# Linear attention ahead of two dense layers: k's projection in plain float32 by row halves, q's maximum subtracted in SBUF, both heads' attend sums in one PSUM bank, closer ranks of units

## The chip, the cores and the metric

One core of one Trainium2 chip. The metric is the device time of one execution in microseconds; below it is the median of three runs.

## What is computed

The inputs are q, k and v (4 batches, 8 heads, 576 positions, 64 features), a feature map w_phi (64 x 128) and the weights of two dense layers, which the kernel receives as 64-bit floats where the host has them so. The output has 2304 rows of 512.

```python
def phi(x):
    proj = np.einsum('bhsd,df->bhsf', x, w_phi)
    proj = proj - np.max(np.abs(proj), axis=-1, keepdims=True)
    return np.concatenate([np.exp(proj), np.exp(-proj)], axis=-1)
q_p, k_p = (phi(q), phi(k))
kv = np.einsum('bhsf,bhsd->bhfd', k_p, v)
z = np.sum(k_p, axis=2)
num = np.einsum('bhsf,bhfd->bhsd', q_p, kv)
den = np.einsum('bhsf,bhf->bhs', q_p, z)[..., None] + 1e-06
x = num / den                         # heads side by side: 2304 x 512
h = np.maximum(np.maximum(x @ w1, x @ w2), x @ w3) @ w_out
...                                   # then rms norm, silu(xn @ w_gate) * (xn @ w_val), @ w_out
```

## The kernel before, in words

**Units.** A unit is two batches and two heads; there are 8 (`NU`). The transposed k and q of a unit are [128, 1152]: rows 0 to 63 are head 0's features, rows 64 to 127 head 1's, and the columns are the positions of both batches. They are cut in 3 chunks of 384 columns (`C`), or 9 blocks of 128.

**The k side of a unit.** A chunk of k comes by two DMAs: `load_k` (L383) on SP's queue into `kraw`, and `load_kh` (L386) on POOL's queue into `kh`, which is float32r (in unit 0, ACT rounds `kraw` into `kh` instead). DVE makes the rest `kl = kraw - kh` (`rest_k`, L389). `k_proj` (L419) multiplies each block by two wide copies of w_phi, `wbh` and `wbl`, with zeros in the other head's quadrants, as three float32r products (`mm3`); both heads' features land side by side in one PSUM bank, two blocks to a bank (ring `pk`, banks 0 and 1). DVE takes the maximum of the absolute values (`k_max`, L429) and subtracts it (`k_sub`, L435), ACT takes the two exponentials (`k_exp`, L443), and `kv_sum` (L445) adds k_p^T [v, 1] of one head in one bank of ring `pkv` (4 and 5). After the last of the 5 steps of a unit `kv_copy` (L458) moves the sums to SBUF (`kvs`).

**The q side of a unit.** For each of 3 chunks `q_proj` (L490) multiplies the two row halves of `qraw` by w_phi in plain float32, head 0 into bank 2 and head 1 into bank 3 (ring `pq`, two banks). ACT copies both to `pc` in SBUF (`q_copy`, L494), POOL finds the largest absolute value over the partitions (`partition_all_reduce`, L498) into `mq`, and DVE's `q_sub` (L503), one per head, reads the projection in PSUM again and writes the difference over `pc`. ACT takes two exponentials (L511). `attend` (L516), one per head, multiplies them by `kvs` into one bank per head of ring `nd` (banks 6 and 7). DVE adds epsilon, inverts and multiplies (`guard` L527, `invert` L532, `divide` L535), per head; PE turns the result (`turn`, L541; ring `xt`, which is bank 1), ACT rounds it to `xh` (L545), and DVE keeps the rest `xl` (L548). A tile of `xh`, `xl` is 384 positions, all features.

**The dense layers.** 64-bit weights come in pieces of 128 x 512, which ACT, DVE and POOL narrow to float32 and split (lines 636 to 673; the first four pieces, which are those of the first layer's first step, go without POOL). Each product is three float32r products through `mm3` (the matmuls of L369 into `up` and `po`). The first `up` depends on `pqlast` (the last `q_proj`) and on `kdone` (nothing of the k side's buffers is used any more).

**What sets the order.** A planner holds a list of operations, each with an engine, a rank, an estimated duration, what it reads and writes, and the ring of buffers that a tile comes from. It plays them through and issues each engine's instructions in the order of their estimated starts; of those that could start within 0.12 us of each other, the lower rank goes first. Each engine then runs its queue in that order. Unit n's ranks begin at n x `U`, with `U = 22.0`; the q side of a unit stands one `U` behind its k side. The loads of the first four weight pieces are ranked at 62, 88, 114 and 140, apart from `U`; all later work of the dense layers is ranked from `A = NU * U + 24`.

```python
for j, r in enumerate(halves):        # q_proj, before and after
    mm(out=buf(f"pq{n}.{c}.{j}")[:, 0:C], lhsT=wst[r, :], rhs=buf(f"qraw{n}.{c}")[r, :], start=True, stop=True)
nc.vector.tensor_tensor(              # q_sub before: first operand in PSUM
    out=buf(f"pc{n}.{c}")[:, j, :], in0=buf(f"pq{n}.{c}.{j}")[:, 0:C], in1=buf(f"mq{n}.{c}")[:, j, :],
    op=ALU.subtract,
)
```

Of the kernel before, what the change touches and what calls it, by code (L numbers as in the profile page):

```python
# [8 lines left out]
FP32 = mybir.dt.float32  # L9
# [8 lines left out]
P = 128  # L18
# [18 lines left out]
NKP = (NST + 1) // 2  # L37
# [162 lines left out]
R384, R256, R512, FULL, HALF = 0.173, 0.118, 0.229, 0.222, 0.15  # L200
# [4 lines left out]
def attn_moe_kernel(ctx, tc, qT, kT, vv, w_phi, w1, w2, w3, wo1, wg, wv, wo2, rms_g, out):  # L205
# [53 lines left out]
    banks("nd", (6, 7))  # L259
    banks("xt", (1,))  # L260
# [8 lines left out]
    ring("kvs", "attnq", 4, [P, 2, 2, 2 * D])  # L269
    ring("den", "attnq", 4, [P, NSUB])  # L270
# [49 lines left out]
    def clear():  # L320
        nc.vector.memset(eps, 1e-6)
        nc.vector.memset(ones, 1.0)
        nc.vector.memset(zero, 0.0)
        for j, r in enumerate(halves):
            for w in (wbh, wbl):
                nc.vector.tensor_copy(out=w[r, (1 - j) * F:(2 - j) * F], in_=zero[r, :])
# [21 lines left out]
    pl.op("DVE", -99, 1.0, clear, w=["zeros", "ones", "eps", "wk"])  # L348
    pl.op("ACT", -98, 1.4, lambda: nc.scalar.activation(out=eps, in_=eps, func=ACTF.Copy), r=["eps"], w=["eps"])
    for j, r in enumerate(halves):  # L350
        f = slice(j * F, (j + 1) * F)
        pl.op("ACT", -97, act_us(F), lambda r=r, f=f: nc.scalar.copy(out=wbh[r, f], in_=wst[r, :]),
              r=["wphi"], w=["wk"])
        pl.op("DVE", -97, dve_us(F), lambda r=r, f=f: nc.vector.tensor_tensor(
            out=wbl[r, f], in0=wst[r, :], in1=r32(wbh[r, f]), op=ALU.subtract), r=["wphi"], w=["wk"])
# [17 lines left out]
    U = 22.0  # L373
    LOAD = 2.5

    def unit(n):
# [532 lines left out]
```

## Time and profile before

| | us |
|---|---|
| median of 3 runs | 953.73 (952.88 to 954.95) |
| the profiled execution | 950.4 |
| its span, first to last instruction | 948.7 |
| PE busy | 924.8 (97%) |
| DVE busy | 611.0 (64%) |
| ACT busy | 346.9 (37%) |
| POOL busy | 254.3 (27%) |

The busy shares are averages over two stages. The attention takes about the first 180 us; the two dense layers take the rest. PE counts as busy while a matmul is in flight, which includes the pipeline's tail behind the last one of a group.

### The profile page before, as it was taken

Reading aid. Unit: us, or ns where it says so; the run is one execution under the profiler, and the core shown is the slowest. Engines: PE = TensorE matmul, PEld = TensorE weight load, DVE = VectorE, ACT = ScalarE, POOL = GpSimd, SP = SyncE. Lnnn points to the kernel's source line nnn. Section 1 sums busy time; section 2 is a strip of 40 time slices with the busy share of each in tenths; the row PEclk is TensorE's granted clock in tenths of the full one; section 3 lists DMA queues with packets and bytes.
Section 4 is the critical chain, followed back from the end, with each engine's and each line's share of the span. In section 5 each row is a group of like instructions: output and inputs, shape, how many; then the busy total and the mean of one; then the engine's idle time right before and its main releaser. Section 6 shows DMA issues by size and latency. Waiting matters only on the chain.

```text
span 948.7 us, 16696 instructions
## 1 busy us (share of the span) xinstructions
PE 924.8 (97%) x6860; PEld 864.1 (91%) x6860; DVE 611.0 (64%) x1160; ACT 346.9 (37%) x645; POOL 254.3 (27%) x184
## 2 busy tenths in 40 slices
PE   8998888899999999999999999999999999999998
PEld 7877776799999999999999999999999999999997
DVE  6899888478856485848788645555645826633233
ACT  6767676455321222213367433123222222211111
POOL 5444443365321231304253123022222202300000
PEclk9999999799999999999999999999999999999999
DMA  8645531023302021201100210200201201000112
GB/s 221 164 125 135 160 99 63 2 67 90 92 20 67 1 67 45 64 26 45 45 1 22 68 44 24 67 18 28 89 1 45 89 1 45 1 1 1 45 68 89
DMA packets 57005, 55.61 MB, mean 59 GB/s; under 512 B 21856, under 2 KB 52320, under 8 KB 56928
## 3 DMA queue, kind: packets, MB, share of 16 engines
q1 hardware_dynamic: 53904, 50.41, 17.8%
q0 software_dynamic: 3024, 4.13, 1.7%
q8 instruction: 54, 0.88, 0.4%
q14 instruction: 23, 0.19, 0.1%
HBM read 49.81 MB, written 4.72 MB: 57 GB/s over the span
## 4 chain that ended last, share of the span: by engine, by line
PE 80%; DVE 1%; issue 0%
PE up L369 55%; PE po L369 23%; DVE xl L814 1%; PE pn L802 0%; PE nd L525 0%; PE pn L791 0%; DVE acc L715 0%; DVE acc L809 0%; PE pq L492 0%; PE xt L543 0%; DVE pc L504 0%; DVE dg L797 0%; DVE hl L739 0%; DVE hf L755 0%; DVE rc L804 0%
## 5 line engine op out<-in xcount | busy, mean ns | idle before, releaser
L369 PE MATMUL up<-xh,wp 128*128 128x384 f32 x2016 | 541.7, 338 | 0.0
L369 PEld LDWEIGHTS up<-xh,wp 128*128 128x128 f32 x2016 | 367.4, 188 | 3.5 <-issue 0.5
L369 PE MATMUL up<-xl,wp 128*128 128x384 f32 x1008 | 340.1, 337 | 0.0
L369 PEld LDWEIGHTS up<-xl,wp 128*128 128x128 f32 x1008 | 189.2, 188 | 2.9
L671 POOL TENSOR_TENSOR wa<-wa,wp 128x512 f32<-128x512 f32 x56 | 80.8, 1443 | 401.0 <-ACT wp L665 335.2
L836 DVE TENSOR_TENSOR hf<-up,hf 128x384 f32<-128x384 f32 x72 | 40.1, 556 | 167.0 <-PE up L369 166.5
L738 ACT CAST hh<-hf 128x384 fp32r<-128x384 f32 x108 | 55.5, 514 | 233.5 <-DVE hf L836 131.7
L369 PE MATMUL po<-wp,hh 128*128 128x512 f32 x432 | 133.6, 390 | 0.0
L715 DVE TENSOR_TENSOR acc<-po,acc 128x384 f32<-128x384 f32 (+1 forms) x210 | 125.3, 610 | 11.9 <-PE po L369 11.6
L834 ACT ACTIVATE hf<-up 128x384 f32<-128x384 f32 x72 | 35.4, 492 | 162.4 <-PE up L369 162.3
L498 POOL PARTITION_ALL_REDUCE mq<-pc x24 | 67.0, 2790 | 95.3 <-issue 61.8
L369 PEld LDWEIGHTS po<-wp,hh 128*128 128x128 f32 x432 | 80.2, 188 | 11.9
L739 DVE TENSOR_TENSOR hl<-hf,hh 128x384 fp32r<-128x384 f32 x108 | 66.9, 620 | 31.9 <-ACT hh L738 31.8
L755 DVE TENSOR_TENSOR hf<-up,hf 128x384 f32<-128x384 f32 x72 | 40.0, 555 | 72.0 <-PE up L369 71.4
L369 PE MATMUL po<-hh,wp 128*128 128x384 f32 x288 | 85.6, 337 | 0.0
L369 PE MATMUL po<-wp,hl 128*128 128x512 f32 x216 | 84.1, 389 | 0.0
L673 POOL TENSOR_TENSOR wp<-wa,wm 128x512 fp32r<-128x512 f32 x56 | 75.2, 1344 | 15.1 <-DVE wm L657 10.1
L369 PEld LDWEIGHTS po<-hh,wp 128*128 128x128 f32 x288 | 53.4, 188 | 0.3
L657 DVE SCALAR_TENSOR_TENSOR wm<-wst,wm 128x512 f32<-128x512 uint32 x60 | 50.6, 844 | 0.9
L636 ACT ACTIVATE wm<-wst 128x512 f32<-128x512 f32 x60 | 40.4, 674 | 29.2 <-POOL wp L673 18.9
L443 ACT ACTIVATE e<-e 128x512 f32<-128x512 f32 (+1 forms) x80 | 45.8, 593 | 12.9 <-DVE e L435 12.1
L369 PE MATMUL po<-hl,wp 128*128 128x384 f32 x144 | 48.6, 338 | 0.1
(81 smaller groups left out, 1059.3 us busy)
## 6 DMA issues: line engine op xcount, KB each, us to landing
wst<-in_moe_w_dram SPq DMA_DIRECT2D x18, 512.0 KB, 3.5
wst<-in_moe_w_out_dram SPq DMA_DIRECT2D x18, 512.0 KB, 3.6
wst<-in_moe_w_gate_dram SPq DMA_DIRECT2D x12, 512.0 KB, 3.6
wst<-in_moe_w_val_dram SPq DMA_DIRECT2D x12, 512.0 KB, 3.6
kraw<-in_kT_dram SPq DMA_DIRECT2D x24, 192.0 KB, 3.2
qraw<-in_qT_dram SPq DMA_DIRECT2D x24, 192.0 KB, 2.7
out_dram<-acc SPq DMA_DIRECT2D x18, 256.0 KB, 2.0
vt<-in_vv_dram SPq DMA_DIRECT2D x16, 256.0 KB, 4.4
```

Of the source, the lines that this page charges most:

```text
L369: mm(out=ps, lhsT=a, rhs=b, start=start and i == 0, stop=stop and i == n - 1)
L443: nc.scalar.activation(out=dst, in_=src, func=ACTF.Exp, scale=-1.0 if u else 1.0)
L498: nc.gpsimd.partition_all_reduce(buf(f"mq{n}.{c}").rearrange("p a c -> p (a c)"), buf(f"pc{n}.{c}").rearrange("p a c -> p (a c)"), P, bass ...
L636: nc.scalar.activation(out=buf(f"wm{self.id}").bitcast(FP32), in_=self.view()[1].bitcast(FP32), func=ACTF.Abs)
L657: nc.vector.scalar_tensor_tensor(out=mf, in0=lo.bitcast(U32), scalar=2.0 ** -52, in1=mf, op0=ALU.mult, op1=ALU.mult)
L671: eng.tensor_tensor(out=a, in0=a, in1=r32(buf(self.h)), op=ALU.subtract)
L673: eng.tensor_tensor(out=buf(self.l), in0=a, in1=buf(f"wm{self.id}").bitcast(FP32), op=ALU.add)
L715: nc.vector.tensor_tensor(out=acc, in0=p, in1=acc, op=ALU.add)
L738: pl.op("ACT", rank, act_us(C), lambda: nc.scalar.copy(out=buf(h), in_=buf(f)), r=[f], w=[h])
L739: pl.op("DVE", rank + 0.6, dve_us(C) + 0.1, lambda: nc.vector.tensor_tensor(out=buf(l), in0=buf(f), in1=r32(buf(h)), op=ALU.subtract), r=[ ...
L755: pl.op("DVE", w + q, dve_us(C), lambda f=f, p=p: nc.vector.tensor_tensor(out=buf(f), in0=buf(p)[:, 0:C], in1=buf(f), op=ALU.max), r=[p], ...
L836: pl.op("DVE", w + q + 4.1, dve_us(C), lambda f=f, p=ups[1]: nc.vector.tensor_tensor(out=buf(f), in0=buf(p)[:, 0:C], in1=buf(f), op=ALU.mu ...
```

## The change

The diff, cut to what acts. k's wide weights, the zeros and the `kh`/`kl` tiles go, with POOL's DMAs of k and DVE's `rest_k`. `k_proj` takes a chunk of three blocks at a time: for each block and head it multiplies 64 rows of `kraw` by 64 rows of w_phi in plain float32, head 0 into bank 0 and head 1 into bank 1. Maximum, difference and exponentials go by chunk and head (384 columns) where they went by two blocks with both heads (512 columns; the fifth step 256). `q_sub` is one instruction of 768 columns for both heads with both operands in SBUF. Both heads' `attend` write one bank (6 x 65 columns of bank 6), and `guard`, `invert` and `divide` are one each for both heads. `xt` has bank 7 for itself. `kvs` and the v tiles are 65 columns wide instead of 128. Ranks are closer: `U` is 17, and chunks stand U/3 apart.

```diff
-    banks("nd", (6, 7))
-    banks("xt", (1,))
+    banks("nd", (6,))
+    banks("xt", (7,))
...
-    ring("kraw", "attnk", 4, [P, C])
-    ring("kh", "attnk", 6, [P, C], FP32R)
-    ring("kl", "attnk", 3, [P, C], FP32R)
-    ring("mk", "attnk", 3, [P, 4])
-    ring("e1", "attnk", 5, [P, 4, F])
-    ring("e2", "attnk", 5, [P, 4, F])
+    ring("kraw", "attnk", 7, [P, C])
+    ring("mk", "attnk", 4, [P, NSUB])
+    ring("e1", "attnk", 9, [P, NSUB, F])
+    ring("e2", "attnk", 9, [P, NSUB, F])
...
-    U = 22.0
+    U = 17
...
-            if n:
-                pl.op("POOL", rk, 0.75, lambda c=c: load_kh(c), w=[kh], size=P * C * 4, lag=LOAD + 1.0, when=hold)
-            else:
-                pl.op("ACT", rk, act_us(C), lambda c=c: nc.scalar.copy(out=buf(f"kh{n}.{c}"), in_=buf(f"kraw{n}.{c}")),
-                      r=[kr], w=[kh])
-            pl.op("DVE", rk + 14, dve_us(C) + 0.4 * (n > 0), lambda c=c: rest_k(c), r=[kr, kh], w=[kl])
...
-        def k_proj(i):
-            pk = buf(f"pk{n}.{i}").rearrange("p (a f) -> p a f", a=2)
-            for t in range(2 * i, min(2 * i + 2, NST)):
-                c, o = divmod(t * P, C)
-                mm3(pk[:, t % 2, :], [(buf(f"kh{n}.{c}")[:, o:o + P], buf(f"kl{n}.{c}")[:, o:o + P], wbh, wbl)])
+        def k_proj(c):
+            for i in range(NSUB):
+                for j, r in enumerate(halves):
+                    mm(out=k_view(c, j)[:, i, :], lhsT=buf(f"kraw{n}.{c}")[r, i * P:(i + 1) * P], rhs=wst[r, :],
+                       start=True, stop=True)
...
+            pk = [new("pk", f"pk{n}.{c}.{j}") for j in range(2)]
+            pl.op("PE", rk - 8, KPROJ, lambda c=c: k_proj(c), r=["wphi", f"kraw{n}.{c}"], w=pk)
...
-        def q_sub(c, j):
-            nc.vector.tensor_tensor(
-                out=buf(f"pc{n}.{c}")[:, j, :], in0=buf(f"pq{n}.{c}.{j}")[:, 0:C], in1=buf(f"mq{n}.{c}")[:, j, :],
-                op=ALU.subtract,
-            )
+        def q_sub(c):
+            pc = buf(f"pc{n}.{c}")
+            nc.vector.tensor_tensor(out=pc, in0=pc, in1=buf(f"mq{n}.{c}"), op=ALU.subtract)
...
-                        mm(out=nd[r, i, 0:D + 1], lhsT=e[:, j, q], rhs=kvs[:, u, b, 0:D + 1], start=u == 0, stop=u == 1)
+                        mm(out=nd[r, 2 * i + j, :], lhsT=e[:, j, q], rhs=kvs[:, u, b, :], start=u == 0, stop=u == 1)
...
-        def divide(c, j):
+        def divide(c):
             nc.vector.tensor_tensor(
-                out=buf(f"xs{n}.{c}")[:, :, j * D:(j + 1) * D], in0=nd_view(c, j)[:, :, 0:D],
-                in1=bc(buf(f"den{n}.{c}.{j}"), [P, NSUB, D]), op=ALU.mult,
+                out=buf(f"xs{n}.{c}").rearrange("p i (j d) -> p (i j) d", j=2), in0=nd_view(c)[:, :, 0:D],
+                in1=bc(buf(f"den{n}.{c}"), [P, 2 * NSUB, D]), op=ALU.mult,
             )
...
-            rk = base + U + 7.3 * c
+            rk = base + U + U / 3 * c
...
-            for j in range(2):
-                pl.op("DVE", rk - 5, dve_us(C), lambda c=c, j=j: q_sub(c, j), r=[pq[j], mq], w=[f"{pc}:{j}"])
+            pl.op("DVE", rk - 5, dve_us(2 * C), lambda c=c: q_sub(c), r=[mq], w=[f"{pc}:0", f"{pc}:1"])
```

## Rows read from the trace of the kernel before

**Rows 1.** The chain of work that ended last, within the first 185 us: start, duration, engine, tile, line, instructions.
```profile
177.16 0.57 DVE pc L504
177.77 1.37 PE pq L492 x4
179.14 2.29 PE up L369 x12
```

**Rows 2.** Busy time of each engine by stretch of the span (instructions in brackets), granted TensorE clock (1.00 is full speed), DMA share, GB/s.
```profile
core 0: us, PE busy (x) PEld busy (x) DVE busy (x) ACT busy (x) POOL busy (x), PEclk, DMA share, GB/s
30.00:50.00 20.00, 20.00 (x360) 16.22 (x360) 16.14 (x39) 15.11 (x30) 8.65 (x6) 1.00 0.53 136
50.00:75.00 25.00, 23.23 (x404) 18.73 (x399) 22.48 (x54) 17.27 (x35) 12.53 (x7) 1.00 0.53 137
75.00:100.00 25.00, 22.52 (x396) 17.68 (x394) 23.77 (x54) 17.49 (x34) 10.28 (x8) 1.00 0.55 138
100.00:125.00 25.00, 22.59 (x379) 18.45 (x379) 21.29 (x49) 17.32 (x34) 9.95 (x7) 0.93 0.51 142
125.00:150.00 25.00, 21.44 (x412) 17.43 (x410) 23.34 (x58) 18.16 (x35) 11.83 (x6) 1.00 0.22 67
160.00:170.00 10.00, 7.67 (x103) 6.02 (x99) 4.09 (x15) 4.97 (x11) 5.09 (x2) 0.67 0.23 73
180.00:220.00 40.00, 40.00 (x310) 39.37 (x309) 27.57 (x54) 19.61 (x39) 19.75 (x13) 1.00 0.18 54
220.00:900.00 680.00, 679.56 (x3716) 654.81 (x3715) 419.32 (x727) 200.07 (x366) 156.49 (x112) 1.00 0.13 39
```

**Rows 3.** POOL's line 498 (the all-reduce over partitions) and ACT's line 459 (the copies of the k sums, two per unit), all of each: duration in ns min/median/max, start of the first and of the last.
```profile
L498 POOL PARTITION_ALL_REDUCE mq<-pc x24: 2734/2737/3202, 13.6 to 180.9; - x24
L459 ACT COPY kvs<-pkv x16: 361/382/403, 18.1 to 161.1; 128x260 f32<-128x260 f32 x16
```

**Rows 4.** The timeline of one turn of the q loop, behind the last k work: start, duration, instruction, idle time before it and its releaser.
```profile
167.65 2.74 POOL L498 PARTITION_ALL_REDUCE mq<-pc  x1 [3.77 <-ACT pc L495]
170.43 1.02 DVE L504 TENSOR_TENSOR pc<-pq,mq 128x384 f32<-128x384 f32 x2 [0.16 <-POOL mq L498]
171.21 1.93 PE L492 MATMUL pq<-qraw,wst 64*128 64x384 f32 x4
173.38 0.84 ACT L495 COPY pc<-pq 128x384 f32<-128x384 f32 x2
174.38 2.74 POOL L498 PARTITION_ALL_REDUCE mq<-pc  x1 [3.99 <-ACT pc L495]
```

**Rows 5.** The timeline of PE: a `q_proj` with both heads, and the first and the last of the six matmuls of one `k_proj` step (two blocks).
```profile
85.01 0.92 PE L492 MATMUL pq<-qraw,wst 64*128 64x384 f32 x4
...
92.75 0.38 PE L369 MATMUL pk<-wbh,kh 128*128 128x256 f32 x1
...
93.44 0.28 PE L369 MATMUL pk<-wbh,kl 128*128 128x256 f32 x1
```

**Rows 6.** Groups of DVE instructions of the first 215 us, shapes apart: count, busy us, mean ns of one, idle time before them.
```profile
L390 DVE TENSOR_TENSOR kl<-kraw,kh 128x384 fp32r<-128x384 f32 x24 | 13.6, 568 | 1.3 <-ACT kh L412 1.1
L429 DVE TENSOR_REDUCE mk<-pk 128x4 f32<-128x512 f32 x32 | 21.7, 685 | 7.1 <-PE pk L369 6.5
L429 DVE TENSOR_REDUCE mk<-pk 128x2 f32<-128x256 f32 x8 | 3.3, 416 | 1.9 <-PE pk L369 1.9
L435 DVE TENSOR_TENSOR e<-pk,mk 128x512 f32<-128x512 f32 x32 | 21.6, 683 | 0.2
L504 DVE TENSOR_TENSOR pc<-pq,mq 128x384 f32<-128x384 f32 x48 | 24.5, 549 | 2.8 <-POOL mq L498 2.8
L528 DVE TENSOR_SCALAR den<-nd 128x3 f32<-128x3 f32 x48 | 7.3, 153 | 15.5 <-PE nd L525 15.4
L533 DVE RECIPROCAL den<-den 128x3 f32<-128x3 f32 x48 | 7.7, 170 | 0.5
L536 DVE TENSOR_TENSOR xs<-nd,den 128x192 f32<-128x192 f32 x48 | 16.0, 351 | 0.5
```

**Rows 7.** Groups of ACT's and POOL's instructions of the first 215 us, in the same columns.
```profile
L443 ACT ACTIVATE e<-e 128x512 f32<-128x512 f32 x64 | 39.5, 635 | 7.4 <-DVE e L435 6.8
L443 ACT ACTIVATE e<-e 128x256 f32<-128x256 f32 x16 | 6.8, 424 | 5.5 <-DVE e L435 5.3
L387 POOL DMA_DIRECT2D kh<-in_kT_dram x21 | 11.9, 567 | 0.0
```

**Rows 8.** The timeline at the start of the attention: k's first chunk rounded, its rest, the first `k_proj`.
```profile
4.69 0.99 ACT L412 CAST kh<-kraw 128x384 fp32r<-128x384 f32 x2 [0.84 <-DMA kraw<-in_kT_dram]
5.24 1.04 DVE L390 TENSOR_TENSOR kl<-kraw,kh 128x384 fp32r<-128x384 f32 x2 [1.06 <-ACT kh L412]
5.40 0.56 PE L369 MATMUL pk<-wbh,kh 128*128 128x256 f32 x1
```

**Rows 9.** The timeline at two places where DVE met an all-reduce, and the spread of durations of four DVE lines (min/median/max ns, start of the first and of the last).
```profile
50.07 2.73 POOL L498 PARTITION_ALL_REDUCE mq<-pc  x1 [4.09 <-issue]
50.23 2.05 DVE L651 SCALAR_TENSOR_TENSOR wa<-wst,wm 128x512 int32<-128x512 int32 x1
...
109.60 2.73 POOL L498 PARTITION_ALL_REDUCE mq<-pc  x1 [4.59 <-issue]
109.62 2.18 DVE L673 TENSOR_TENSOR wp<-wa,wm 128x512 fp32r<-128x512 f32 x1
...
L651 DVE SCALAR_TENSOR_TENSOR wa<-wst,wm x6: 676/688/2047, 50.2 to 153.3; 128x512 int32<-128x512 int32 x6
L673 DVE TENSOR_TENSOR wp<-wa,wm x4: 674/1254/2182, 65.4 to 143.6; 128x512 fp32r<-128x512 f32 x4
L390 DVE TENSOR_TENSOR kl<-kraw,kh x24: 540/549/780, 5.2 to 142.1; 128x384 fp32r<-128x384 f32 x24
L504 DVE TENSOR_TENSOR pc<-pq,mq x46: 539/548/559, 16.3 to 177.6; 128x384 f32<-128x384 f32 x46
```

**Rows 10.** The timeline of PE: the loads of weights and the matmuls of another `q_proj`, whose two banks came free one after the other; each line of loads is one row half's two.
```profile
91.44 0.29 PEld L492 LDWEIGHTS pq<-qraw,wst 64*128 64x128 f32 x2 [1.14 <-DVE pc L504]
91.45 1.37 PE L492 MATMUL pq<-qraw,wst 64*128 64x384 f32 x4 [1.00 <-DVE pc L504]
91.91 0.29 PEld L492 LDWEIGHTS pq<-qraw,wst 64*128 64x128 f32 x2 [0.17 <-DVE pc L504]
```

More of the change, by code (lines that the diff above doesn't have):

```diff
@@ L322, in clear @@
         nc.vector.memset(ones, 1.0)
[L323 to L326, printed above, removed]
     def identity():
@@ L347, in attn_moe_kernel @@
     pl.op("PE", -101, 4.0, wake, r=["ones2"], w=[new("nd", "wake")])
-    pl.op("DVE", -99, 1.0, clear, w=["zeros", "ones", "eps", "wk"])
+    pl.op("DVE", -99, 0.3, clear, w=["ones", "eps"])
     pl.op("ACT", -98, 1.4, lambda: nc.scalar.activation(out=eps, in_=eps, func=ACTF.Copy), r=["eps"], w=["eps"])
[L350 to L355, printed above, removed]
     for i in range(2):
@@ L428, in k_max, with k_view @@
-        def k_max(i, nt):
+        def k_proj(c):
[3 more added lines that the diff above has]
+                       start=True, stop=True)
+        def k_view(c, j):
+            return buf(f"pk{n}.{c}.{j}")[:, 0:C].rearrange("p (a f) -> p a f", f=F)
+        def k_max(c, j):
             nc.vector.tensor_reduce(
-                out=buf(f"mk{n}.{i}")[:, 0:2 * nt], in_=k_view(i, nt), axis=AX.X, op=ALU.max,
-                apply_absolute_value=True,
+                out=buf(f"mk{n}.{c}.{j}"), in_=k_view(c, j), axis=AX.X, op=ALU.max, apply_absolute_value=True,
@@ L432, in k_max, with k_sub @@
             )
-        def k_sub(i, nt):
+        def k_sub(c, j):
             nc.vector.tensor_tensor(
-                out=buf(f"e2{n}.{i}")[:, 0:2 * nt], in0=k_view(i, nt),
-                in1=bc(buf(f"mk{n}.{i}")[:, 0:2 * nt], [P, 2 * nt, F]), op=ALU.subtract,
-            )
-        def k_exp(i, nt, u):
-            src = buf(f"e2{n}.{i}")[:, 0:2 * nt]
-            dst = src if u else buf(f"e1{n}.{i}")[:, 0:2 * nt]
+                out=buf(f"e2{n}.{c}.{j}"), in0=k_view(c, j), in1=bc(buf(f"mk{n}.{c}.{j}"), [P, NSUB, F]), op=ALU.subtract,
+            )
@@ L443, in k_exp, with kv_sum @@
+        def k_exp(c, j, u):
+            src = buf(f"e2{n}.{c}.{j}")
+            dst = src if u else buf(f"e1{n}.{c}.{j}")
             nc.scalar.activation(out=dst, in_=src, func=ACTF.Exp, scale=-1.0 if u else 1.0)
-        def kv_sum(i, nt, j):
-            ps = buf(f"pkv{n}.{j}").rearrange("p (u b f) -> p u b f", u=2, b=2)
-            for t in sorted(range(2 * i, 2 * i + nt), key=lambda t: t == MIX):
+        def kv_sum(c, j):
+            ps = buf(f"pkv{n}.{j}")[:, 0:4 * (D + 1)].rearrange("p (u b f) -> p u b f", u=2, b=2)
+            for t in sorted(range(NSUB * c, NSUB * c + NSUB), key=lambda t: t == MIX):
@@ L452, in kv_sum @@
                         if t == MIX:
-                            mm(out=ps[r, u, :, 0:D + 1], lhsT=e[:, r], rhs=vm[:, j], start=first, stop=last)
+                            mm(out=ps[r, u], lhsT=e[:, r], rhs=vm[:, j], start=first, stop=last)
                         else:
                             b = int(t > MIX)
-                            mm(out=ps[r, u, b, 0:D + 1], lhsT=e[:, r], rhs=vt[:, t - b, j, 0:D + 1], start=first, stop=last)
+                            mm(out=ps[r, u, b, :], lhsT=e[:, r], rhs=vt[:, t - b, j, :], start=first, stop=last)
@@ new lines, in kv_copy @@
+                out=buf(f"kvs{n}.{j}").rearrange("p u b f -> p (u b) f"),
+                in_=buf(f"pkv{n}.{j}")[:, 0:4 * (D + 1)].rearrange("p (a f) -> p a f", a=4),
+            )
+        for c in range(NCH):
+            rk = base + U / 3 * c
+            pk = [new("pk", f"pk{n}.{c}.{j}") for j in range(2)]
+            pl.op("PE", rk - 8, KPROJ, lambda c=c: k_proj(c), r=["wphi", f"kraw{n}.{c}"], w=pk)
+            for j in range(2):
+                x = 0.5 * j
+                mk = new("mk", f"mk{n}.{c}.{j}")
+                e1, e2 = new("e1", f"e1{n}.{c}.{j}"), new("e2", f"e2{n}.{c}.{j}")
+                pl.op("DVE", rk - 7 + x, dve_us(C), lambda c=c, j=j: k_max(c, j), r=[pk[j]], w=[mk])
+                pl.op("DVE", rk - 6.9 + x, dve_us(C), lambda c=c, j=j: k_sub(c, j), r=[pk[j], mk], w=[e2])
+                pl.op("ACT", rk - 5 + x, act_us(C), lambda c=c, j=j: k_exp(c, j, 0), r=[e2], w=[e1])
+                pl.op("ACT", rk - 4.9 + x, act_us(C), lambda c=c, j=j: k_exp(c, j, 1), w=[e2])
+                if c == 0:
+                    new("pkv", f"pkv{n}.{j}")
+                kv = f"pkv{n}.{j}"
+                vr = ([2], [0, 1, 2, 3], [3])[c]
+                pl.op("PE", rk + j, NSUB * 2 * HALF, lambda c=c, j=j: kv_sum(c, j),
```

82 lines of the change are left out of this document (26 added, 56 removed).

## The prediction

> **What bounds the kernel now.** I read the chain that ended last first. It runs on PE through the dense layers back to 179.1 us; there it goes from the first `up` to the last `q_proj` and to the `q_sub` before that [rows 1]. The stretches say why: from 180 us on PE is busy in 40.00 of 40 and in 679.56 of 680 us at full clock [rows 2]. So the time is the moment at which the dense layers may start, here 179.1 us, plus a PE queue of 769.6 us that the change does not touch. A microsecond gained ahead of that moment is a microsecond of the kernel; one gained behind it is nothing.
>
> What sets 179.1? The all-reduces of the q side: 24 of them between 13.6 and 180.9 us, one every 7.3 us [rows 3], though each takes 2.7. One turn of their loop, where nothing else is left to do, shows the reason [rows 4]: all-reduce 2.74, two `q_sub` 1.02, `q_proj` 1.93 (begun behind the first of them), copies 0.84, and the next all-reduce, 6.7 us after the last one. `q_sub` reads the projection in PSUM, `pq` has one bank per head, so chunk c+1 cannot be projected before chunk c is subtracted. From 161 us, when the last k sums are copied [rows 3], this loop runs alone: PE's clock is down at 0.67 in between, and DVE is busy 4.09 of 10 us [rows 2]. Ahead of that the loop is not alone: from 50 to 150 us PE is busy for 89.8 us, DVE for 90.9, ACT for 70.2 [rows 2]. Two limits, then: crowded engines until the k side ends, and the bare loop behind it.
>
> **The change part by part.** The profiled execution took 950.4 us, the median of the runs is 953.7; I make the sum in the profile's time and carry the difference over to the median.
>
> *Crowded stretch.* The k sums of units 0 and 7 are copied at 18.1 and 161.1 us, 20.4 us per unit [rows 3]. At the shares of 50 to 150 us a unit holds 18.3 us of PE, 18.5 of DVE and 14.3 of ACT.
>
> PE: six matmuls of `k_proj` take 0.97 us from the first start to the last end, so nine, a chunk's worth, take 1.46 [rows 5]. The new form streams the same 2 x 384 columns through two row halves in plain float32 as a `q_proj` does, which takes 0.92 [rows 5]. That is 1.6 us per unit less, PE 16.7. No row shows the short form with new weights every 128 columns. Below, 0.92 is the least I can defend; above, halves that run one after the other make it 1.84. I take 0.92: `q_proj` is nearest in type, row halves and banks.
>
> DVE: per unit `rest_k` 3 x 0.568, `k_max` and `k_sub` 4 x (0.685 + 0.683) + 2 x 0.416, `q_sub` 6 x 0.549, the divisions 6 x (0.153 + 0.170 + 0.351) [rows 6] make 15.3 us. After it: twelve k steps of 384 columns at 0.55 (midway between 512 and 256) 6.6; three `q_sub` of 768 at 0.95 (0.549 and 384 more columns at 0.269 per 256) 2.9; `guard` and `invert` 3 x 0.32, `divide` 3 x 0.55. That is 12.1, so 3.2 less: 15.3 us per unit.
>
> ACT: eight exponentials at 0.635 and two at 0.424 [rows 7] become twelve at 0.53: 0.4 us more, 14.7.
>
> PE is now the fullest. At the 0.91 that DVE, the fullest before, reached, a unit takes 18.3 us; were PE never idle, as between 30 and 50 us (20.00 of 20 [rows 2]), 16.7. Seven units at 2.1 less: **14.7 us**. The start gives **1 us**: the first k chunk need not be rounded and split between its landing at 4.7 and `k_proj` at 5.4 [rows 8].
>
> *Behind the k side.* `pq` is now free once ACT has copied it, so the loop is cut. Alone, a chunk costs PE 0.92 + 1.6 + 0.55, ACT about 3.0 and POOL 2.74: some 3.1 us in place of 6.7. Three `pc` buffers let `q_proj` run one or two chunks ahead. From the last k copy to the last `q_proj` there were 18 us; I take two chunks, 6 us (one gives 3, the old backlog of three with a wait 12). **12 us** less. One more `attend` and `turn` then stand behind the start of the dense layers: **2 us** given back.
>
> *At nothing.* POOL loses 21 DMA issues, 11.9 us [rows 7], on an engine that idles anyway; SP keeps its 24 loads of k, earlier through seven buffers. One `nd` bank makes `attend` of the next chunk wait for `divide` of this one, and `guard` for both heads: 1.6 + 0.2 + 0.9 us once per chunk of 6.1, covered unless DVE is 3 us late; it would be paid by PE's queue, where the k work of the next unit stands. `k_proj` needs both its banks at once and waits for head 1's `k_sub`; a turn of that is 0.92 and four DVE steps, 3.3 us, again inside 6.1. `xt` no longer shares a bank with k. Closer ranks make nothing shorter; they give the order.
>
> *The sum.* 14.7 + 1 + 12 - 2 = 25.7 us: 950.4 becomes 924.7, and the median **928.0**.
>
> *A rule against it.* Where a DVE instruction with both operands in SBUF starts just after an all-reduce, it lasts 2.05 us (its median is 0.69) or 2.18 (least 0.67); it gets going 1.5 us after the all-reduce began [rows 9]. `q_sub` with its PSUM operand never did: 539 to 559 ns over 46 of them [rows 9]. The new one can. The sum holds nothing for it: all-reduces 6.1 us apart leave about 3 us between the end of one, which releases `q_sub`, and the start of the next. The Trainium skill, "SBUF — State Buffer", section "SBUF: two separate sides", says that the pair of ports shared by VectorE and GpSimd is locked for the whole instruction. The trace disagrees on how long: 1.5 of 2.7 us.
>
> **The rivals.**
>
> *k's projection stays as dear (B).* If a row half's loads do not hide behind its matmuls, the six loads in series of a chunk add 5 x 0.10 us (the second load of a pair starts 0.10 after the first [rows 10]): 1.42 us, the old cost; serial halves cost 1.84. PE then holds 18.2 to 19.4 us, a unit 20.0 to 21.4, and with the 1 + 12 - 2 of the other terms the median is 940 to 950. For it: two loads per half in a row are all that `q_proj` shows. Against it: k's old matmuls, with new weights every time, start 0.14 us apart on average [rows 5]. By the Trainium skill, "TensorE: Matmul & The Clock Gate", section "Part 3: Packing small matmuls — row/col tiling", loads overlap matmuls in flight only in another row group; no row here decides that.
>
> *`q_sub` held by the next all-reduce, slower (C).* If the loop, once cut, bunches the all-reduces back to back, each `q_sub` starts as the next one begins. Held 1.4 us each, DVE has 19.5 us per unit, a unit takes 21.4, and the gain behind the k side leaves 950. Held through the whole 2.6 us, DVE has 23.1, a unit 25.4: 35 us lost against 11 gained, about 978. It turns slower at 1.6 us per `q_sub`, beyond the 1.5 of the rows; three `pc` buffers, each returned by an `attend`, space the all-reduces.
>
> *The gain is given back at the first layer (D).* The last DVE step of the fourth weight piece is at 143.6 us [rows 9], its rank stays while the attention shrinks. If it slips behind the earlier start, the first `po` waits, up to 10 us: 935 to 945. Against it: the first two `up` need pieces that were done long before.
>
> **How the numbers follow.** The forecast has 0.70, its own range 914 (PE never idle, 3 us behind the k side) to 938. B 0.17, D 0.06, C 0.07. The range 915 to 945 leaves out C, the dearest part of B and the far end of the forecast, under 2 in 10 together. A measurement of this kernel can tell 0.2%, about 2 us, from no change. Faster: all of the forecast, 0.14 of B, 0.05 of D: 0.89. Same: 0.04. Slower: C, 0.07.
>
> **What would show it.** The dense layers' first `up` at 150 to 155 us, and the last `q_proj` no longer behind a `q_sub`. All-reduces about 6 us apart until the last k copy, near 145 us, then about 3. DVE's `q_sub` at 0.95 us, with few over 1.5. `k_proj` of a chunk in 0.9 us; 1.4 or more means B. If the all-reduces still stand 7 us apart, the loop was not the limit and the forecast is wrong. The PE queue behind the first `up` should still be 770 us; a longer one means D.

## The result, and the profile after

| | before | after |
|---|---|---|
| median of four runs, us | 953.37 (952.88 to 954.95) | 911.14 (909.01 to 912.27) |
| the profiled execution | 950.4 | 909.01 |
| its span | 948.7 | 907.1 |

The ratio is 0.9552, 95% interval 0.9531 to 0.9573: 42 us less. The forecast was 928.0 with a range of 915 to 945, so the sign was right and the size was not.

The chain that ended last comes to the dense layers 41.5 us earlier than [rows 1]. Start, duration, engine, tile, line:

```profile
133.15 0.95 PE pq L460 x2
134.10 0.83 PE xt L509 x3
134.94 2.65 PE nd L491 x48
137.59 4.36 PE up L353 x24
```

Behind its first `up` the span goes on for 907.1 - 137.6 = 769.5 us; before it was 948.7 - 179.1 = 769.6. All of the gain lies ahead of the dense layers. By stretch, with the columns of [rows 2]:

```profile
50.00:75.00 25.00, 23.43 (x521) 20.12 (x521) 22.89 (x50) 23.09 (x47) 12.46 (x5) 1.00 0.50 136
75.00:100.00 25.00, 25.00 (x552) 21.46 (x547) 21.48 (x48) 22.07 (x47) 12.21 (x5) 1.00 0.53 137
100.00:125.00 25.00, 24.17 (x535) 20.67 (x535) 23.03 (x50) 23.38 (x49) 13.71 (x5) 1.00 0.24 74
```

From 50 to 125 us PE is busy for 97%, DVE for 90 and ACT for 91; before it was 91, 90 and 69. This looks like a kernel that its engines fill. The all-reduces and the copies of the k sums, as in [rows 3], give the pace:

```profile
L466 POOL PARTITION_ALL_REDUCE mq<-pc x24: 2741/2741/2998, 13.1 to 136.0; - x24
L427 ACT COPY kvs<-pkv x16: 352/377/400, 16.7 to 128.2; 128x260 f32<-128x260 f32 x16
```

The all-reduces stand (136.0 - 13.1)/23 = 5.34 us apart, where they stood 7.27 apart; a unit takes (128.2 - 16.7)/7 = 15.9 us in place of 20.4. Now one turn of the loop, which answers to [rows 4] (lines of other work left out):

```profile
73.51 2.74 POOL L466 PARTITION_ALL_REDUCE mq<-pc  x1 [2.71 <-DVE mk L399]
...
76.28 0.96 DVE L473 TENSOR_TENSOR pc<-pc,mq 128x768 f32<-128x768 f32 x1
...
77.28 0.85 ACT L477 ACTIVATE eq<-pc 128x768 f32<-128x768 f32 x1 [0.57 <-DVE pc L473]
...
78.03 0.84 ACT L463 COPY pc<-pq 128x384 f32<-128x384 f32 x2
...
78.96 2.74 POOL L466 PARTITION_ALL_REDUCE mq<-pc  x1 [2.71 <-ACT pc L463]
```

The next chunk's `q_proj` ran beside `q_sub` and the start of the exponential (76.63 to 77.55), and nothing of the loop waited for it. Yet its copies stand behind the first exponential in ACT's queue, that one waits for `q_sub`, and `q_sub` waits for the all-reduce. So all-reduce, `q_sub`, exponential and copies are still in series: 2.74 + 0.96 + 0.84 + 0.84 and the gaps between them are 5.45 us, and 11 of the 23 distances between all-reduces are 5.45 to the hundredth. The loop was not cut; it lost `q_proj`, an exponential and part of its waits: before, the copies stood behind both exponentials in all 23 turns, now they stand between the two in 20 and ahead of both in 3.

The new forms of `k_proj` and `q_proj` on PE, beside [rows 5] (a plain float32 matmul of the program shows as two records, so these are two and six matmuls):

```profile
76.63 0.92 PE L460 MATMUL pq<-qraw,wst 64*128 64x384 f32 x4
...
77.38 0.83 PE L392 MATMUL pk<-wst,kraw 64*128 64x128 f32 x12
```

DVE's groups up to 175 us, beside [rows 6]: count, busy us, mean ns, idle time before them.

```profile
L404 DVE TENSOR_TENSOR e<-pk,mk 128x384 f32<-128x384 f32 x48 | 25.1, 549 | 0.1
L399 DVE TENSOR_REDUCE mk<-pk 128x3 f32<-128x384 f32 x48 | 24.6, 550 | 10.6 <-PE pk L392 10.3
L473 DVE TENSOR_TENSOR pc<-pc,mq 128x768 f32<-128x768 f32 x24 | 24.2, 1010 | 5.3 <-POOL mq L466 5.1
L502 DVE TENSOR_TENSOR xs<-nd,den 128x384 f32<-128x384 f32 x24 | 13.3, 555 | 0.5
L499 DVE RECIPROCAL den<-den 128x6 f32<-128x6 f32 x24 | 4.5, 186 | 0.3
L494 DVE TENSOR_SCALAR den<-nd 128x6 f32<-128x6 f32 x24 | 3.8, 158 | 2.2 <-PE nd L491 2.2
```

The durations on which the DVE sum rested were as forecast to within 0.03 us, but for `q_sub`: its median is 0.96 us for the forecast 0.95, its mean 1.01, since two of the 24 took 1.32 and 1.96.

### The profile page after: what moved, and what is told of

Its sections match the earlier page's. It is cut to its first block, busy times and chain, and to the rows that moved or that the text cites. A ratio compares the mean times of both kernels' runs of the same rounds, so it can differ in the third digit from the quotient of the medians.

```text
span 907.1 us, 16682 instructions
## 1 busy us (share of the span) xinstructions
PE 894.8 (99%) x6932; PEld 846.3 (93%) x6932; DVE 583.9 (64%) x1049; ACT 344.1 (38%) x656; POOL 241.4 (27%) x163
## 4 chain that ended last, share of the span: by engine, by line
PE 91%; DVE 4%; POOL 1%; ACT 1%; SPq 1%; issue 1%; DMA 1%; POOLq 0%
PE up L353 58%; PE po L353 24%; PE nd L491 3%; PE pkv L424 2%; PE pq L460 1%; POOL mq L466 1%; PE pk L392 1%; PE xt L509 1%; DVE xl L779 1%; DVE pc L473 1%; DMA qraw<-in_qT_dram 1%; PE pkv L421 0%; DVE wm L608 0%; PE pn L767 0%; DVE mk L399 0%
## 5 line engine op out<-in xcount | busy, mean ns | idle before, releaser
L704 DVE TENSOR_TENSOR hl<-hf,hh 128x384 fp32r<-128x384 f32 x108 | 68.4, 633 | 32.1 <-ACT hh L703 32.1
L411 ACT ACTIVATE e<-e 128x384 f32<-128x384 f32 x96 | 46.8, 525 | 8.7 <-DVE e L404 7.2
L353 PE MATMUL po<-hl,wp 128*128 128x384 f32 x144 | 48.6, 338 | 0.1
```

Source lines behind the costliest of these rows:

```text
L353: mm(out=ps, lhsT=a, rhs=b, start=start and i == 0, stop=stop and i == n - 1)
L704: pl.op("DVE", rank + 0.6, dve_us(C) + 0.1, lambda: nc.vector.tensor_tensor(out=buf(l), in0=buf(f), in1=r32(buf(h)), op=ALU.subtract), r=[ ...
```

## The experiments

Theory L: the time ahead of the dense layers is 24 turns of the q loop, and a turn is as long as what the queues put in series in it. Its rival is the forecast's own reasoning (theory E), that the engines' load sets the pace of the crowded stretch. Each run stands beside runs of the kernel before on the same chip (medians 953.3 to 955.6); ratios are against those.

The mean turn of each kernel (the 4th to the 23rd), worked out from the starts and ends of the instructions in its trace, in us. "Late" is the time from the end of the step before it in the turn to its own start, in which its engine may be busy with other work; the next chunk's copies are counted from the end of the first exponential to their own end (negative: done before it).

| kernel | median | all-reduce | `q_sub` late | `q_sub` | exp late | exp | copies | turn |
|---|---|---|---|---|---|---|---|---|
| before | 953.4 | 2.80 | 0.45 | 1.03 | 0.11 | 0.85 | 1.83 | 7.26 |
| after | 911.1 | 2.76 | 0.14 | 1.00 | 0.07 | 0.84 | 0.41 | 5.32 |
| a1_sub_only | 943.8 | 2.92 | 1.27 | 0.97 | 0.19 | 0.85 | 0.85 | 7.14 |
| a2_sub_psum | 941.4 | 2.86 | 0.14 | 1.02 | 0.04 | 0.84 | 1.73 | 6.80 |
| a3_old_ranks | 940.3 | 2.78 | 0.46 | 1.02 | 0.15 | 0.84 | 1.49 | 6.83 |
| a4_old_k | 928.1 | 2.90 | 0.65 | 1.02 | 0.14 | 0.84 | 0.55 | 6.24 |
| b1_ranks_only | 948.8 | 2.82 | 0.44 | 1.01 | 0.06 | 0.84 | 1.76 | 7.10 |
| n1_two_nd_banks | 924.4 | 2.85 | 0.51 | 1.12 | 0.33 | 0.85 | -0.03 | 5.75 |
| b2_kv_six_of_nine | 910.5 | 2.76 | 0.13 | 1.01 | 0.05 | 0.84 | 0.38 | 5.30 |
| b3_half_reduce | 904.7 | 1.58 | 1.33 | 0.95 | 0.21 | 0.84 | 0.54 | 5.03 |
| b4_copies_ahead | 909.9 | 2.75 | 0.38 | 1.03 | 0.76 | 0.85 | -0.41 | 5.44 |
| v1_ranks_16_copies_ahead | 909.8 | 2.78 | 0.49 | 1.02 | 0.94 | 0.85 | -0.73 | 5.44 |
| d1_exps_together | 930.1 | 2.79 | 0.08 | 1.03 | 0.05 | 0.84 | 1.24 | 6.13 |
| d2_old_ranks_copies_between | 939.0 | 2.82 | 0.89 | 0.94 | 0.24 | 0.85 | 0.99 | 6.82 |
| w1_old_ranks_new_holds | 917.6 | 2.80 | 1.19 | 1.06 | 0.21 | 0.84 | -0.57 | 5.66 |
| w2_new_ranks_old_holds | 938.9 | 2.79 | 0.32 | 0.95 | 0.11 | 0.84 | 1.77 | 6.88 |

(What is missing to the turn is 0.1 to 0.2 us from the copies to the next all-reduce; in b3 the next all-reduce starts 0.43 us ahead of the end of the second copy.) Across these kernels a longer turn goes with a longer time: 23 turns of 1.94 us more are 45 us, and before is 42 slower than after. Elsewhere this is rougher (by its turn a1 would stand at 953), since the turns at either end and the queue behind the first `up` differ too.

### One part alone, one part taken out

**a1_sub_only**: the kernel before with `q_sub` in SBUF and nothing else.

```diff
-            for j in range(2):
-                pl.op("DVE", rk - 5, ..., q_sub(c, j), r=[pq[j], mq], w=[f"{pc}:{j}"])
+            pl.op("DVE", rk - 5, ..., q_sub(c), r=[mq], w=[f"{pc}:0", f"{pc}:1"])
```

> The kernel before with one part of the change alone: q_sub as one instruction with both operands in SBUF (k side, divisions, banks and ranks are the old ones). Theory L (the time ahead of the dense layers is set by the q loop; the change shortens the loop from 6.5 us, all-reduce, two subtractions, projection, copies, to 5.45 us, all-reduce, subtraction, first exponential, copies in ACT's order): the loop no longer binds and the old k side's load does, 6.1 to 6.5 us per chunk, so 926 to 936 us. Theory E (the engines' load is what counted, so the k part made the gain): 945 us or more.

943.75 us, ratio 0.9877 (0.9858 to 0.9896): between the two, nearer the rival. L missed here: I had taken the loop as shortened everywhere. The copies do come earlier (0.85 in place of 1.83), but `q_sub` then stands 1.27 us late, behind k's steps and the divisions on a DVE that is busy for 93% of 50 to 100 us (92% before), and the turn stays at 7.14.

**a2_sub_psum**: the changed kernel with `q_sub` reading PSUM again, one per head (the reverse of the diff above).

> The changed kernel with q_sub put back as two instructions that read the projection in PSUM; all else is the new form. Theory L: the loop is 6.5 us again, 23 turns at 1.1 us more than the 5.4 of the changed kernel are 26 us, so 934 to 941 us, all-reduces 6.5 to 6.7 us apart. Theory E: the load is that of the changed kernel, so 911 to 918 us.

941.42 us, 0.9855 (0.9835 to 0.9875), 0.4 us above L's range and far from E's: `q_proj` again waits for `q_sub`, the copies end 1.73 us behind the exponential. Its busy times teach more than its time:

```profile
50.00:75.00 25.00, 24.45 (x482) 19.77 (x481) 22.78 (x52) 20.35 (x42) 10.40 (x4) 1.00 0.35 99
75.00:100.00 25.00, 23.90 (x516) 20.17 (x515) 22.19 (x49) 20.45 (x46) 11.22 (x4) 1.00 0.53 141
100.00:125.00 25.00, 22.43 (x436) 18.22 (x434) 19.60 (x43) 19.36 (x41) 9.99 (x4) 0.93 0.26 77
```

PE's instructions per unit are those of the changed kernel. From 50 to 125 us a2 has 1423 records of matmuls (of `attend` 506, of k sums 672), the changed kernel 1598 (672 and 670). PE is busy for 70.8 us in a2, for 72.6 there: 11% fewer matmuls, 2.5% less busy time. A part of this is the clock, granted at 0.93 in a2's last stretch; but in the 50 us at full clock, too, 993 records take 48.4 us in a2 and 1065 take 48.4 there. A busy PE is not a loaded PE.

**a3_old_ranks**: the changed kernel with the old spacing.

```diff
-    U = 17
+    U = 22.0
...
-            rk = base + U / 3 * c - 32          # k loads; likewise q: base + U + 7.3 * c
+            rk = base + 7.3 * c - 32
```

> The changed kernel with the old ranks: U = 22 and chunks 7.3 apart. Theory L: the loop is made of the same instructions, so 911 to 917 us. Rival (the closer ranks made part of the gain by another order of the instructions): 920 us or more.

940.33 us, 0.9839 (0.9813 to 0.9866): the rival was right. Closer ranks, which the prediction put at nothing, are worth 27 us in the presence of the rest (0.9839 - 0.9552 of 953.4).

**a4_old_k**: the changed kernel with k's side as before (`kh`, `kl`, three products, steps of 512 columns); the 128 columns of the v tiles and the planner's estimate for small matmuls (0.15 us in place of 0.13) are the old ones with it.

> The changed kernel without its k part: k by two DMAs, split and projected in three float32r products, five steps per unit with both heads; q_sub in SBUF, one nd bank and closer ranks as in the changed kernel. Theory L: the loop of 5.45 us would allow 911, but DVE and PE hold some 6 us per chunk with the old k side, so 922 to 932 us. Theory E: nearly the whole gain is gone, 940 us or more.

928.06 us, 0.9714 (0.9694 to 0.9735), within L's range. Here an engine is near its limit, DVE, the third busy time of each line (48.6 of 50 us):

```profile
50.00:75.00 25.00, 25.00 (x456) 20.33 (x455) 23.95 (x45) 19.21 (x38) 13.26 (x8) 1.00 0.55 146
75.00:100.00 25.00, 25.00 (x467) 20.21 (x465) 24.69 (x46) 20.89 (x42) 12.99 (x8) 1.00 0.59 159
```

Not all of it lies in the turns. The first `up` comes at 147.9 us, and behind it the span of 926.3 us goes on for 778.4, some 9 us more than in the changed kernel: the `attend` of three chunks stands there in place of two, and PE waits 4.3 us for DVE's divisions.

**b1_ranks_only**: the kernel before with `U = 17` and chunks U/3 (k steps U/5) apart.

> The kernel before with the closer ranks alone (U = 17, chunks U/3 and k steps U/5 apart). Theory L (the q loop, and above it the order of the queues, sets the pace): the loop through the projection's PSUM banks stays at 6.5 us, so all-reduces 6.5 to 7 us apart and 938 to 950 us. Rival O (the order alone is worth what the changed kernel lost with the old ranks, 29 us): 920 to 930 us.

948.81 us, 0.9941 (0.9919 to 0.9963), within L's range. Alone the ranks give 6 us: `q_proj` still waits for `q_sub` in PSUM.

**n1_two_nd_banks**: the changed kernel without its third part.

```diff
-    banks("nd", (6,))
-    banks("xt", (7,))
+    banks("nd", (6, 7))
+    banks("xt", (1,))
...
-        def divide(c):          # guard, invert likewise
+        def divide(c, j):
```

> The changed kernel without its third part: each head's attend sums in a bank of their own (6 and 7) again, guard, invert and divide per head, xt again in bank 1, which k's projection uses. Theory L: the loop stays, with two turns in which the copies stand behind both exponentials (2 us), and DVE gets 6 x 0.67 - 3 x 0.90 = 1.3 us more per unit, which 10% idle covers mostly: 911 to 917. Rival X (the one bank for both heads is what let the units close up, since xt no longer stops k's projection): 922 to 935.

924.43 us, 0.9685 (0.9660 to 0.9711): L's 911 to 917 was too low, the low end of X's range holds. The part is worth 13 us, and the prediction had put it at nothing. One place of its trace, cut to four lines:

```profile
61.35 5.46 POOL L466 PARTITION_ALL_REDUCE mq<-pc  x2 [3.50 <-DVE wm L622]
...
64.12 2.44 DVE L473 TENSOR_TENSOR pc<-pc,mq 128x768 f32<-128x768 f32 x1
...
67.73 1.01 DVE L404 TENSOR_TENSOR e<-pk,mk 128x384 f32<-128x384 f32 x2
...
68.38 2.12 PE L392 MATMUL pk<-wst,kraw 64*128 64x128 f32 x12 [2.42 <-issue]
```

Two all-reduces back to back hold a `q_sub` for 1.5 us, and PE idles 2.4 us ahead of a `k_proj`. What it waits for at this place is not `xt`, which shares bank 1 with it, but the chunk before: its `k_sub` (67.73) stood behind the held `q_sub` in DVE's queue, and `k_proj` starts 0.1 us after the first head's `k_sub` has ended. The k side ends last in this kernel: the last k sums are copied at 151.5 us and the first `up` follows at 153.0, while the last all-reduce began at 147.3. How the 13 us divide between the bank, DVE's 1.3 us more per unit and such holds was not tried.

By the ratios, taking out `q_sub` costs 29 us, the ranks 27, k's side 15 and the `nd` bank 13: 84 together, though the whole change gained 43. Alone, `q_sub` gave 12 and the ranks 6. The parts don't add up: each is worth little until the others have gone out of the turn's way.

### Load or loop

**b2_kv_six_of_nine**: the changed kernel, with the k sums leaving out blocks 1, 3 and 7 of 9.

```diff
+                if t in (1, 3, 7):
+                    continue
```

> The changed kernel whose k sums leave out three of the nine blocks of a unit (blocks 1, 3 and 7): 16 of 48 matmuls per chunk on average less for PE, some 0.5 us per chunk; order and loop as they are. Theory L (the loop all-reduce, subtraction, exponential, copies sets 5.45 us): no change, 908 to 912 us. Theory E (PE, busy 97% of 50 to 125 us, sets the pace): 23 x 0.5 us less, 899 to 902 us.

910.47 us, 0.9542 (0.9523 to 0.9560). A third less of the k sums moved nothing; PE's busy time from 50 to 125 us fell to 68.4 us, and the mean turn was 5.30: PE's load is not the limit of the changed kernel.

```profile
50.00:125.00 75.00, 68.41 (x1380) 56.92 (x1376) 67.71 (x147) 68.73 (x142) 37.99 (x15) 1.00 0.42 115
```

**b3_half_reduce**: the changed kernel, with the all-reduce over head 0's columns only, whose maximum serves both heads.

```diff
-                buf(f"mq{n}.{c}").rearrange(...), buf(f"pc{n}.{c}").rearrange(...), P,
+                buf(f"mq{n}.{c}")[:, 0, :], buf(f"pc{n}.{c}")[:, 0, :], P,
```

> The changed kernel whose all-reduce takes the maximum of head 0's 384 columns alone, subtracted from both heads (head 1's own maximum is left out): the loop is shorter by what the all-reduce loses, 1.2 to 1.4 us, and PE, DVE and ACT have the same work in the same order. Theory L: the pace falls until another engine binds (DVE and ACT hold 4.9 to 5.0 us per chunk), 899 to 905 us. Theory E: no change, 909 to 912 us.

904.68 us, 0.9484 (0.9458 to 0.9510), as L has it. POOL is busy for only half of the time, and yet a shorter all-reduce (1.54 us) shortens the kernel by 6.5 us. The edit shortens the loop by more than that: the all-reduce no longer reads head 1's columns, and in each of the 20 turns it starts 0.09 us after head 0's copy, without waiting for the second. The gain is not 24 x 1.2 = 29 us: the turn became 5.03, `q_sub` now standing 1.33 us late behind other work of DVE, PE busy throughout and ACT for 95%. So the loop is the changed kernel's limit, but the engines' own work, as it is queued, lies only 0.3 us per turn below it:

```profile
50.00:75.00 25.00, 24.96 (x568) 21.78 (x567) 23.02 (x51) 24.11 (x49) 7.71 (x5) 1.00 0.50 137
75.00:100.00 25.00, 25.00 (x543) 21.30 (x541) 22.48 (x51) 23.31 (x49) 7.71 (x5) 1.00 0.54 143
100.00:125.00 25.00, 24.96 (x558) 21.04 (x552) 22.94 (x53) 23.57 (x49) 7.09 (x5) 1.00 0.23 68
```

**d1_exps_together**: the changed kernel; the planner's order is altered so that each second exponential of q stands directly behind the first.

```diff
+        for c in range(3 * NU):
+            order.remove(at["F", c])
+            order.insert(order.index(at["E", c]) + 1, at["F", c])
```

> The changed kernel with ACT's order altered in one point: each second exponential of q stands directly behind the first, so that the two copies of the next chunk stand behind both in 20 of 23 turns (in the changed kernel: between the two exponentials in 20, ahead of both in 3). Theory L (the q loop sets the time; one turn is all-reduce 2.74, q_sub 0.96, the exponentials that stand ahead of the next copies, the copies 0.84): each such turn is one exponential, about 0.93 us, longer, 6.38 in place of 5.45, so 17 to 20 us: 926 to 931. Rival P (what the queue order of ACT is does not matter; the old ranks cost time in another way): 909 to 914.

930.12 us, 0.9747 (0.9729 to 0.9765), as L has it. No engine does more or less than in the changed kernel; one exponential more stands ahead of two copies, and this turn is 6.39 us:

```profile
97.86 2.74 POOL L471 PARTITION_ALL_REDUCE mq<-pc  x1 [3.65 <-DVE mk L404]
100.64 0.96 DVE L478 TENSOR_TENSOR pc<-pc,mq 128x768 f32<-128x768 f32 x1 [1.48 <-POOL mq L471]
101.63 0.84 ACT L482 ACTIVATE eq<-pc 128x768 f32<-128x768 f32 x1 [1.68 <-DVE pc L478]
102.56 0.84 ACT L482 ACTIVATE pc<-pc 128x768 f32<-128x768 f32 x1
103.31 0.84 ACT L468 COPY pc<-pq 128x384 f32<-128x384 f32 x2
104.25 2.74 POOL L471 PARTITION_ALL_REDUCE mq<-pc  x1 [3.64 <-ACT pc L468]
```

### What the ranks do

**d2_old_ranks_copies_between**: a3 with the copies moved ahead of the second exponential where what they need stands ahead of it.

```diff
+                if order.index(i) > spot and all(order.index(k) < spot for k in ...):
+                    order.remove(i)
+                    order.insert(spot, i)
```

> The changed kernel with the old ranks (U = 22, chunks 7.3 apart), and with the copies of the next chunk moved ahead of the second exponential in ACT's queue wherever what they need stands ahead of it: between the exponentials in 16 turns, ahead in 3, behind both in 4 (under the old ranks without the move: 17 behind both). Theory L (the ranks matter through that place): 13 turns get 0.93 us shorter each, 12 us or more of the 29 that the old ranks cost: 922 to 929. Rival R (the old ranks cost by the distance of the k side from the q side or another order, not by the copies): 936 to 941.

939.03 us, 0.9843 (0.9821 to 0.9865): L's number missed, R's held. The copies came 0.5 us nearer (0.99 in place of 1.49), and `q_sub` got 0.43 us later. One of its turns, lines of other work left out:

```profile
139.40 2.74 POOL L480 PARTITION_ALL_REDUCE mq<-pc  x1 [5.41 <-ACT pc L477]
143.00 0.94 DVE L487 TENSOR_TENSOR pc<-pc,mq 128x768 f32<-128x768 f32 x1
143.21 0.92 PE L474 MATMUL pq<-qraw,wst 64*128 64x384 f32 x4
143.98 0.84 ACT L491 ACTIVATE eq<-pc 128x768 f32<-128x768 f32 x1
145.14 0.84 ACT L477 COPY pc<-pq 128x384 f32<-128x384 f32 x2
146.07 3.32 POOL L480 PARTITION_ALL_REDUCE mq<-pc  x1 [3.93 <-DVE wm L624]
```

The all-reduce ends at 142.14, `q_sub` starts 0.9 us later, behind other work of DVE, and `q_proj` (143.21 to 144.13) ends behind the start of the exponential. Over the 4th to the 23rd turn `q_proj` ends 0.43 us behind the start of the exponential, and in 7 of the 20 behind its end; in the changed kernel it ends 0.43 us ahead of that start, and never behind that end. The old ranks hurt in three queues, DVE's, PE's and ACT's.

**w1_old_ranks_new_holds** and **w2_new_ranks_old_holds** separate the two things that `U` sets: the rank, and the earliest times at which the planner lets a unit's loads begin (hold times). w1 is a3 with these times from 17; w2 is the changed kernel with those from 22:

```diff
-                  when=max(0.0, base + 5.0 * c - 30))          # base = 17 * n
+                  when=max(0.0, 22 * n + 5.0 * c - 30))        # v and q likewise
```

> The changed kernel with the old ranks (U = 22, chunks 7.3 apart) for every operation, but with the earliest times at which the planner lets a unit's loads of k, v and q begin taken from U = 17. In ACT's queue the next chunk's copies then stand ahead of both exponentials in 10 turns, between them in 5 and behind both in 8 (old ranks: 3, 3, 17; changed kernel: 3, 20, 0). Theory H (the old ranks cost through these hold times: the planner counts on loads 22 us per unit apart and orders the queues for a slower pace than the chip's): most of the 29 us come back, 8 turns at 0.93 us are left: 915 to 924. Theory R (the rank itself, by which work is chosen when several instructions could start, decides): 934 to 941.

> The changed kernel with its own ranks (U = 17), but with the earliest times at which the planner lets a unit's loads of k, v and q begin taken from U = 22. In ACT's queue the next chunk's copies then stand ahead of both exponentials in 1 turn, between them in 11 and behind both in 11. Theory H (hold times): 11 turns at 0.93 us by the copies alone, 921, and with the places of q_proj and q_sub as under the old ranks up to 940: 921 to 940. Theory R (the rank itself): as the changed kernel but for the copies, 909 to 921.

w1 917.63 us, 0.9618 (0.9597 to 0.9638); w2 938.93, 0.9838 (0.9820 to 0.9857): theory H, twice. By w1, 21 of the 27 us lie in the hold times; by w2, all of them. They are no waits on the chip: they are times in the planner's own reckoning, and with loads 22 us per unit apart it lays out queues for a pace that the chip no longer has. In w2 the copies end 1.77 us behind the exponential, and `q_proj` ends behind it in 7 of 20 turns. That they stand behind work that was planned to be over is my reading; no run shows it.

### The copies still further ahead

**b4_copies_ahead** ranks `q_proj` and its copies 17 ahead of the chunk in place of 9; **v1_ranks_16_copies_ahead** takes `U = 16` besides.

```diff
-            pl.op("PE", rk - 9, 0.84, lambda c=c: q_proj(c), ...)      # and q_copy
+            pl.op("PE", rk - 17, 0.84, lambda c=c: q_proj(c), ...)
```

> The changed kernel with projection and copies of q ranked 8 us earlier: in ACT's queue the copies of the next chunk then stand ahead of the first exponential of this one for 14 of 24 chunks, where 4 did. Theory L: the loop is open for half the chunks, 900 to 909 us. Theory E: no change, 909 to 913 us; the new order may cost something elsewhere in either.

> The changed kernel with ranks still closer (U = 16) and q_proj with its copies ranked 17 ahead of the chunk in place of 9, so that the copies stand ahead of both exponentials in 18 of 23 turns and between them in 5. Theory L with ACT, PE and DVE close behind (all over 90% busy): the loop alone would allow 4.5 us per turn, the engines about 5.2, as with the halved all-reduce: 902 to 909. Rival F (the engines' own work fills the 5.4 already): 909 to 912.

909.89 us (909.27 to 910.25) and 909.84 (909.28 to 910.45), ratios 0.9537 (0.9519 to 0.9555) and 0.9535 (0.9514 to 0.9556): not told from the changed kernel. The copies are out of the loop (done 0.41 and 0.73 us before the exponential ends), but the exponential now starts 0.76 and 0.94 us late, behind other work of ACT, and the turn is 5.44. The loop's numbers missed in both, the rivals' held. What was gained ahead of the dense layers was also given back behind their start. The matmuls into `up` (line 353), in the changed kernel and then in b4: durations in ns, start of the first and of the last:

```profile
L353 PE MATMUL up<-xh,wp x2016: 333/336/633, 137.5 to 896.3; 128*128 128x384 f32 x184
L353 PE MATMUL up<-xh,wp x2016: 333/336/633, 135.0 to 897.3; 128*128 128x384 f32 x184
```

The first `up` comes 2.5 us earlier (in v1 2.7), but the span goes on behind it for 908.1 - 135.0 = 773.1 us (v1 the same), 3.5 more: the `attend` of three chunks stands there in place of two, and PE idles 1.1 us longer, waiting for DVE's divisions.

## Why the prediction was wrong

**The bound** was named rightly: the start of the dense layers plus a queue of 769.6 us that stays (769.5).

**The crowded stretch** is the step that failed, by its size: 7 units at 2.1 us, 14.7, measured 7 x (20.4 - 15.9) = 31.5. The working took PE's busy time per unit for its load (18.3 - 1.6 = 16.7) and divided by the 0.91 that the fullest engine had reached. Both halves were wrong. The load: a2 shows PE busy for more time per matmul when it is not pressed, so 16.7 is no floor, and the unit came to 15.9. I had read that off 20.00 of 20 us [rows 2]; busy time says only that some matmul was in flight. The share: 0.91 was what engines reach while a loop holds them. The Trainium skill, "Perfetto Trace Analysis", section "Identifying the Most-Contended Engine", says that the busy share of matmuls is no good measure of how close a kernel is to the limit, and offers the arithmetic done, as a share of the peak, and the busy share of weight loads in its place. The trace agrees on the first: 70.8 us in a2 against 72.6 in the changed kernel. The loads' 58.2 against 62.3 us follow the work better, 7% less for the 11% fewer matmuls.

**The loop** "is cut", said the prediction, and so left it out of the crowded stretch and gave it 3.1 us behind the k side. Freeing `pq` cut `q_proj` loose, but ACT's queue still ties the copies to the exponential: 5.45 us. From the rows at hand that was 2.74 [rows 4], 0.95 for `q_sub` [rows 6], an exponential of 768 columns (0.84 measured; [rows 7] have 0.635 for 512) and 0.84 for the copies [rows 4]. Three turns of it are 16.35 us, which is what the unit became, within 0.4.

**Closer ranks make nothing shorter; they give the order.** The second half was right and refutes the first: the order sets the loop's length. a3 gives 27 us for it, and w1 and w2 put most of that on the planned hold times.

**The start** gave 1.4 us (1 forecast; first k copy at 16.7 for 18.1). **Behind the k side** 18.0 us became 9.4, so 8.6 for 12: the last three all-reduces stand 5.8 and 2.8 us apart, where 3 was forecast, and the chain from the last `q_proj` to the first `up` goes through a `turn` and one chunk's `attend`, which took 2.65 us at a granted clock of 0.83 (130 to 140 us) and takes 1.55 at full clock (142.28). **Given back**: 2 were forecast; as before, the `attend` of two chunks stands behind the first `up`, and the queue there did not grow, so nothing. In all 31.5 + 1.4 + 8.6 = 41.5.

**At nothing** stood the one `nd` bank, too: 13 us (n1).

**The rivals.** B fell: a chunk's `k_proj` takes 0.83 us in 20 of 24 cases, so the loads hid. D fell: the queue behind the first `up` did not grow. (In a4, b4 and v1 it did, by 3.5 to 9 us: more `attend` stood behind it, and PE waited for DVE's divisions.) C's mechanism is there, but rare. In the changed kernel:

```profile
133.19 5.81 POOL L466 PARTITION_ALL_REDUCE mq<-pc  x2 [2.77 <-ACT pc L463]
133.44 2.16 DVE L616 SCALAR_TENSOR_TENSOR wa<-wst,wm 128x512 int32<-128x512 int32 x1
136.79 1.96 DVE L473 TENSOR_TENSOR pc<-pc,mq 128x768 f32<-128x768 f32 x1
```

This is the longest `q_sub` of the 24, where one all-reduce follows the other directly. The loop itself guards the rest: 2.7 us lie between all-reduces. L616, which began 0.25 us into an all-reduce, lasted 2.16 us in place of 0.69, so it was held for 1.5 us of the 2.9. By the Trainium skill, "SBUF — State Buffer", section "SBUF: two separate sides", it would have been held until the all-reduce had ended; here the trace does not agree.

## What to carry to other kernels

Before dividing busy time by a share, write out the shortest turn of every loop that passes through several engines, with the place of each instruction in its queue, and compare it with the measured pace: an engine that is 91% busy may be stretched over a loop. Freeing a buffer cuts a loop only as far as the queues let the next turn run ahead; look which instruction stands ahead of the freed one. When a change makes part of a planned program faster, the plan's own pace (its hold times and estimates) has to follow, or the queues keep the old one.

## What the runs showed of the hardware

An all-reduce over 128 x 768 takes 2.74 us and over 128 x 384 takes 1.54 (b3), so the second 384 columns cost 1.20. The six matmuls of a `k_proj` chunk in plain float32 (twelve records), with new weights each time and two row halves side by side, end 0.83 us after the first starts; a `q_proj`, of the same columns with a third as many loads, takes 0.92. Two row halves with six records of loads each thus cost no more than two with two. A DVE instruction with both operands in SBUF that started 0.25 us into an all-reduce took 2.16 us in place of 0.69, so it was held, but not until the all-reduce's end.
